# Windowed attention and a gated feed-forward in one kernel: half units, finer score bursts, and a planned choice of engines

## The chip, the cores and the metric

The kernel runs on one core of one Trainium2 chip. A core has five engines with a queue of instructions each, taken in order: PE (TensorE, matmuls), DVE (VectorE), ACT (ScalarE), POOL (GpSimd) and SP (SyncE, which here only starts DMA transfers). They meet through semaphores. PE and the vector engines exchange data through PSUM, eight banks of 128 x 512 fp32; everything else lies in SBUF, 128 partitions wide. The metric is the device time of one execution in microseconds (us), the median of several runs.

## The reference

Attention with a causal window of 64 positions, eight batches, eight heads, 576 positions, head size 64, all fp32; its output is the input of a feed-forward of width 1024 with a three-tap convolution along the sequence as a gate. The three weights arrive as 64-bit floats.

```python
def _attn_ref(q, k, v) -> np.ndarray:
    scores = scale * np.matmul(q, k.transpose(0, 1, 3, 2))
    mask = (rel >= 0) & (rel < window)
    scores = np.where(mask, scores, -1000000000.0)
    attn = np.exp(scores - np.max(scores, axis=-1, keepdims=True))
    attn = attn / (np.sum(attn, axis=-1, keepdims=True) + 1e-09)
    return np.matmul(attn, v).astype(np.float32)

def _moe_ref(x, w_in, conv_w, w_out) -> np.ndarray:
    h = np.maximum(x @ w_in, 0.0)
    ...
    for k in range(K):
        conv_out += conv_w[k][None, None, :] * hp[:, k:k + S, :]
    gate = 1.0 / (1.0 + np.exp(-conv_out))
    return (h * gate @ w_out).astype(np.float32)
```

## The kernel before

The 8 x 576 = 4608 positions are cut into twelve **units** of 384 (six blocks of 64, `NT`), u = 0 to 11. A unit passes through two parts.

**Attention.** `softmax` handles twelve pairs (head group g, block t) in three **bursts** of four (`NB`). `qk` (L347) multiplies queries and keys into PSUM on PE, `row_max` (L360, DVE) adds the mask and takes the row maximum, `exps` (L369, ACT) computes the exponentials, two instructions for each block, with the row sum beside, `guard` and `reciprocal` prepare the divisor, `normalise` (L382) multiplies, on DVE for units 0 to 2 and on POOL later. The probabilities are then turned. For units 0 and 1 ("wide", `BY_PE`) PE transposes them (`transpose_pe`, L389) and ACT copies them back (`untile`, L394). For the later units DVE transposes squares of 32 (`transpose`, L410) and small DMAs bring them to their place (`place`). `values` (L484) multiplies with v, one of four column groups c at a time; `split_hi` (ACT) and `split_lo` (DVE) write the result x as the sum of two reduced-precision numbers, xh and xl.

**Feed-forward** (`moe`, L573). The 1024 columns of DFF are eight steps f of 128. `mm1` (L505) computes one step as twelve matmuls of 128 x 128 by 384 columns (four c, three products: xh times the high weight, xh times the low one, xl times the high one) into one of two `acc` banks. `relu` (ACT) brings it to `hbuf`. For each pair i of steps `carry` (POOL) brings over the columns at the unit's edge, `conv_mid` (ACT) and `conv_side` (DVE, twice) form the convolution, `sig` (ACT), `gate` (DVE), `gate_hi` (ACT) and `gate_lo` (DVE) make the gated values gh and gl. `mm2` (L565) multiplies them with w_out into four banks `po`, summing over all eight steps; it runs about five steps (`LAG`) behind mm1. Then `po` is copied out (L607, L609) and stored.

**Weights.** Each of the sixteen chunks (eight of w_in, eight of w_out, 128 x 512) is loaded as 64-bit words of 0.5 MB into a staging tile, `bits`, of which there are two (each two chunks wide, and overlapping the tiles T of the transposes and of the output). `to_f32` (L248) turns them into fp32: ACT takes the absolute value of the high words (L252), POOL a maximum with a tiny number (L253), DVE shifts (L254) and puts in the sign (L256), ACT scales the low words (L259), DVE adds them (L260). `weights` then rounds to the high part (POOL for w_in, L277, ACT for w_out, L275) and DVE subtracts for the low part (L278). All eight steps of unit 0 come before unit 1, so all sixteen chunks are needed within unit 0.

**Order.** Every operation is a `Work` with a due time t (the tables START) and a cost. `queued` (L61) simulates the five engines with these costs and writes out the order in which each engine's instructions are issued; on the chip each queue then runs in that order and waits where data is late. Where the simulated PE would stand still in the first 110 us, `keep_busy` (L209) puts in matmuls on a tile of zeros (L216). ACT needs a table load when it changes between exponential and sigmoid (ACT_TABLE_LOAD in the profile).

Of the kernel before, what the change touches and what calls it, by code (L numbers as in the profile page):

```python
# [28 lines left out]
LAG = 5  # L29
BY_PE = 2  # L30
NB = 4
NBU = 2 * NT // NB
MASKED = -8.0e9
TINY = 2.0 ** -15

LAST = NU - 1
# [10 lines left out]

class Work:


    def __init__(self, t, eng, cost, do, r, w, kind, mb, port):
        self.t, self.eng, self.cost, self.do, self.r, self.w, self.kind, self.mb = t, eng, cost, do, r, w, kind, mb
        self.port = port
        self.needs, self.after, self.ready = 0, [], 0.0
        self.start = self.end_ = 0.0


def queued(works, fill=None):  # L61

    import heapq
    writer, readers = {}, {}
    for x in works:
        deps = set()
        for k in x.r:
            if k in writer:  # L70
                deps.add(writer[k])
        for k in x.w:
            deps.update(readers.get(k, ()))
            if k in writer:
                deps.add(writer[k])
        deps.discard(x)
        for d in deps:
            d.after.append(x)
        x.needs = len(deps)
# [4 lines left out]
    free = {"PE": 0.0, "DVE": 0.0, "ACT": 2.0, "POOL": 0.7, "SP": 1.3}  # L84
    state = dict.fromkeys(free)
    waiting = {e: [] for e in free}
    touched = {k: ("", 0.0) for k in [("sc", 0)] + [("acc", i) for i in range(2)] + [("po", i) for i in range(NC)]}
    for x in works:
        if x.needs == 0:
            waiting[x.eng].append(x)  # L90
    dma, port, order, left = 0.0, {"DVE": 0.0, "POOL": 0.0}, [], len(works)
    while left:
        best = None
        for e, ws in waiting.items():
            if not ws:
                continue
            start = max(free[e], min(x.ready for x in ws))
            if best is None or start < best[0]:
                best = (start, e)
        start, e = best  # L100
        x = min((x for x in waiting[e] if x.ready <= start),
                key=lambda x: x.t - (0.5 if x.kind and x.kind == state[e] else 0.0))
        if x.port:
            if e == "POOL" and start < port["DVE"]:
                free[e] = port["DVE"]
                continue
            start = max(start, port["POOL"])
            port[e] = start + x.port
        waiting[e].remove(x)
        if fill and e == "PE" and start < FILL_TO:  # L110
            t = max(free[e], FILL_FROM)
            n = int((start - t) * FILL)

            clean = [(end, k) for k, (by, end) in touched.items() if by != "PE" and end < t]
            if n > 0 and clean:
                order.append(Work(x.t, e, 0.0, fill(n, min(clean)[1]), [], [], None, 0, 0.0))
        turn = SWITCH[e] if e in SWITCH and (x.kind != state[e] if e == "PE" else x.kind and x.kind != state[e]) else 0.0
        if turn and e == "PE" and not x.kind:
            turn = LEAVE
        if e == "PE" or x.kind:  # L120
            state[e] = x.kind
        end = free[e] = start + turn + x.cost * (1.75 if e == "PE" and start < WARM else 1.0)
        if x.mb:
            dma = max(dma, start) + x.mb * 2.7
            end = dma + 1.9
        for k in x.r + x.w:
            if k in touched:
                touched[k] = e, end
        order.append(x)
        left -= 1  # L130
        for y in x.after:
            y.needs -= 1
            y.ready = max(y.ready, end + (0.0 if e == "PE" else 0.06) if y.eng == e else end + 0.2)
            if y.needs == 0:
                waiting[y.eng].append(y)
    return order

START = {  # L140
    "v0": -34.213,
    "pv0": -15.486,
    "conv": -34.622,
    "bits": ((-44.162, -48.108), (-49.962, -46.523)),
    "qk1": -44.058,
    "v1": -6.318,
    "qk2": 0.918,
    "qk0": (-88.698, -55.197, -55.435),
    "ex0": (-38.484, -35.539, -25.91),
    "sc1": (-35.664, -14.916, -14.661),  # L150
    "ex1": (-10.948, -3.722, -2.234),
    "mask": -13.894,
    "sig": ((5.143, 6.743, 8.637, 10.624), (2.954, 4.077, 7.59, 9.996), (4.046, 6.806, 8.285, 10.314)),
    "in": (-40.063, -38.679, -33.327, -12.569, -5.818),
    "out": (-5.241, -4.847, 7.996, 9.148),
# [13 lines left out]
def attention_moe(ctx: ExitStack, tc: tile.TileContext, q, k, v, w_in, conv_w, w_out, out):  # L169
# [56 lines left out]
    def two(t, eng, cost, do, **kw):  # L226
        at(t, eng, cost, do, port=cost, **kw)
# [74 lines left out]

    def wide(u):
# [429 lines left out]
```

## Time and profile before

| | |
|---|---|
| median of 3 runs | 529.05 us (527.6 to 529.41) |
| the profiled execution, its span | 528.6 us |
| busy: PE, DVE, ACT, POOL | 507.8, 377.7, 384.5, 105.5 us |
| matmuls (PE instructions) | 5646 |
| moved by DMA | 69.94 MB |

The span is that of one execution taken by the profiler. Busy time counts an engine's instructions only, not its waits; a busy PE may also be running at a lower clock, or on filler matmuls. A group's row reads: line, engine, operation, what is written and read, shapes, count, then total busy time, mean duration in ns, and the idle time just before these instructions with what ended it. In the chain of waits each piece of time belongs to what the end was waiting for. A row of the timeline begins with start and duration.

### The profile page before, as it was taken

To read this page: it belongs to the slowest core of one execution; us is meant where nothing else is said; L and a number is where in the kernel's file an instruction comes from. 1 tells how busy PE (TensorE), PEld (TensorE's weight loads), DVE (VectorE), ACT (ScalarE), POOL (GpSimd) and SP (SyncE) were. 2 spreads that over 40 slices of the span, in tenths; PEclk is the share of its full clock that TensorE was granted. 3 is DMA by queue.
4 is the path that set the end of the run, shared out by engine and by line. 5 is a ranking of instruction groups with operands and counts; after the bars stand their busy time and mean duration, and the time that the engine had idled before them with its cause. 6 is when DMAs were issued, how large, how long until landed. Compare 5 with 4: busy or idle time off the path is not lost.

```text
span 528.6 us, 14478 instructions
## 1 busy us (share of the span) xinstructions
PE 507.8 (96%) x5646; PEld 486.1 (92%) x5646; DVE 377.7 (71%) x1084; ACT 384.5 (73%) x1017; POOL 105.5 (20%) x192
## 2 busy tenths in 40 slices
PE   6867899999999999999999999999999999999996
PEld 4657799999899999999999999999999999999996
DVE  3998999998668676667767767767767767655552
ACT  1988999788795994696696697687687687544541
POOL 5663645112011120011021021021021021000000
PEclk9998999999999999999999999999999999999999
DMA  8982670265472264172173073083073053010011
GB/s 275 378 276 101 231 258 2 51 203 190 115 269 68 66 206 129 56 275 69 40 288 77 22 256 112 23 287 97 14 279 99 24 165 95 13 61 1 1 61 60
DMA packets 29459, 69.94 MB, mean 132 GB/s; under 512 B 5712, under 2 KB 17616, under 8 KB 29392
## 3 DMA queue, kind: packets, MB, share of 16 engines
q1 hardware_dynamic: 29392, 69.03, 39.6%
q8 instruction: 44, 0.72, 0.6%
q14 instruction: 23, 0.19, 0.1%
HBM read 47.73 MB, written 9.47 MB: 108 GB/s over the span
## 4 chain that ended last, share of the span: by engine, by line
PE 89%; DMA 4%; ACT 3%; DVE 2%; issue 1%; SPq 0%; ACTq 0%
PE po L571 39%; PE acc L508 38%; PE acc L488 6%; PE sc L357 5%; DMA q<-in_q_dram 2%; DMA T<-in_w_in_dram 1%; DVE s L364 1%; ACT ub L396 1%; ACT s L374 0%; ACT w L252 0%; DVE wil L278 0%; DVE w L260 0%; DVE xl L495 0%; DVE s L385 0%; ACT L374 0%
## 5 line engine op out<-in xcount | busy, mean ns | idle before, releaser
L508 PE MATMUL acc<-xh,wih 128*128 128x384 f32 x384 | 132.2, 344 | 1.8 <-ACT hbuf L529 0.9
L542 DVE SCALAR_TENSOR_TENSOR c<-hbuf,cw,c 128x386 f32<-128x386 f32 (+1 forms) x192 | 110.0, 624 | 32.8 <-ACT c L535 32.7
L571 PE MATMUL po<-gh,woh 128*128 128x386 f32 (+1 forms) x384 | 132.3, 345 | 0.0
L508 PE MATMUL acc<-xh,wil 128*128 128x384 f32 x384 | 130.9, 341 | 0.0
L508 PE MATMUL acc<-xl,wih 128*128 128x384 f32 x384 | 130.6, 340 | 0.0
L571 PE MATMUL po<-gh,wol 128*128 128x386 f32 (+1 forms) x384 | 129.8, 338 | 0.0
L571 PE MATMUL po<-gl,woh 128*128 128x386 f32 (+1 forms) x384 | 129.8, 338 | 0.0
L374 ACT ACTIVATE s<-s,nm 128x96 f32<-128x96 f32 (+2 forms) x288 | 105.4, 370 | 5.1 <-DVE nm L364 4.9
L508 PEld LDWEIGHTS acc<-xh,wih 128*128 128x128 f32 x384 | 72.9, 190 | 3.5 <-issue 2.1
L562 DVE TENSOR_TENSOR gl<-c,gh 128x772 fp32r<-128x772 f32 (+1 forms) x48 | 54.9, 1144 | 28.6 <-ACT gh L558 28.3
L571 PEld LDWEIGHTS po<-gh,woh 128*128 128x128 f32 x384 | 72.2, 188 | 2.9
L508 PEld LDWEIGHTS acc<-xl,wih 128*128 128x128 f32 x384 | 73.0, 190 | 0.0
L508 PEld LDWEIGHTS acc<-xh,wil 128*128 128x128 f32 x384 | 72.9, 190 | 0.0
L385 POOL TENSOR_TENSOR s<-s,r 128x768 f32<-128x768 f32 x27 | 39.7, 1471 | 165.4 <-DVE r L380 154.1
L554 DVE TENSOR_TENSOR c<-c,hbuf 128x772 f32<-128x772 f32 (+1 forms) x48 | 47.0, 980 | 36.0 <-ACT c L549 35.9
L571 PEld LDWEIGHTS po<-gl,woh 128*128 128x128 f32 x384 | 72.3, 188 | 0.0
L571 PEld LDWEIGHTS po<-gh,wol 128*128 128x128 f32 x384 | 72.3, 188 | 0.0
L529 ACT ACTIVATE hbuf<-acc 128x384 f32<-128x384 f32 x64 | 30.8, 484 | 46.2 <-PE acc L508 45.9
L549 ACT ACTIVATE c<-c 128x772 f32<-128x772 f32 (+1 forms) x48 | 40.7, 848 | 27.4 <-DVE c L542 27.2
L364 DVE CUSTOM_DVE_ANT_0 s<-sc,mask 128x96 f32<-128x96 f32 (+2 forms) x272 | 51.6, 254 | 9.0 <-POOL mask L328 5.3
L374 ACT ACTIVATION_READ_ACCUMULATOR s<-s,nm 128x1 f32 x288 | 55.2, 192 | 0.0
L535 ACT ACTIVATE c<-hbuf,cw 128x386 f32<-128x386 f32 (+1 forms) x96 | 53.6, 609 | 0.0
(64 smaller groups left out, 576.2 us busy)
## 6 DMA issues: line engine op xcount, KB each, us to landing
v<-in_v_dram SPq DMA_DIRECT2D x24, 768.0 KB, 7.1
ub<-T SPq DMA_DIRECT2D x240, 48.0 KB, 2.0
k<-in_k_dram SPq DMA_DIRECT2D x22, 448.0 KB, 5.6
q<-in_q_dram SPq DMA_DIRECT2D x22, 384.0 KB, 5.8
out_dram<-T SPq DMA_DIRECT2D x8, 772.0 KB, 4.4
T<-in_w_in_dram SPq DMA_DIRECT2D x8, 512.0 KB, 6.9
T<-in_w_out_dram SPq DMA_DIRECT2D x8, 512.0 KB, 5.1
out_dram<-T SPq DMA_DIRECT2D x3, 768.0 KB, 6.2
```

The source lines that it names most:

```text
L364: nc.vector.tensor_tensor_reduce(out=ss[b][:, i, h, o:n], in0=banks_of(u, b)[h][:, i * P + o:i * P + n], in1=mask[m][:, o:n], scale=-0.125 ...
L374: nc.scalar.activation(x, x, AF.Exp, bias=nms[b][:, e], scale=-1.0, accum_out=sms[b][:, e])
L385: on.tensor_tensor(sv, sv, rs[b].unsqueeze(2).broadcast_to([P, 2 * NB, n]), ALU.mult)
L488: nc.tensor.matmul(acc[bank(("v", u, c))][h * D:(h + 1) * D, t * W:(t + 1) * W], vs[:, c, t, h], ub[g][:, 2 * p:2 * p + 2, 2 * t + h], sta ...
L508: nc.tensor.matmul(acc[bank(("m", u, f))][:, :NX], w[:, f, c], x[u % 2][:, c], start=(c == 0 and j == 0), stop=(c == NC - 1 and j == 2))
L529: nc.scalar.activation(hbuf[:, f, o:o + NX], ps[:, :NX], AF.Relu)
L535: nc.scalar.activation(cs[i % 2][:, a, :n], hbuf[:, f, 1:1 + n], AF.Copy, scale=cw[:, 1, f:f + 1])
L542: nc.vector.scalar_tensor_tensor(c, hbuf[:, f, e:e + n], cw[:, e, f:f + 1], c, op0=ALU.mult, op1=ALU.add)
L549: nc.scalar.activation(c, c, AF.Sigmoid)
L554: nc.vector.tensor_tensor(c, c, hbuf[:, 2 * i:2 * i + 2, 1:1 + n], ALU.mult)
L562: nc.vector.tensor_tensor(gls[ring(u, i)][:, :, :n], cs[i % 2][:, :, :n], ghs[ring(u, i)][:, :, :n].bitcast(F32), ALU.subtract)
L571: nc.tensor.matmul(po[o][:, :n], w[:, f, es], x, start=(f == 0 and j == 0), stop=(f == NF - 1 and j == 2))
```

## The change

The whole body is rewritten around a plan; these are its parts.

- **Half units.** Units 0 and 1 run the feed-forward in two halves of DFF each, in turn: unit 0 steps 0 to 3, unit 1 steps 0 to 3, unit 0 steps 4 to 7, unit 1 steps 4 to 7 (`TASKS`). Each half sums its own `po` banks and copies them out. The first half is stored; the second is added to it in DRAM by an accumulating DMA that POOL issues (`store_more`). xh and xl of both units are held until then. Eight more copies out of PSUM result.
- **Bursts of two.** For units 0 and 1 a burst is two pairs instead of four (`FINE`, `bursts`), six bursts a unit. Their q and k come from one new input, `first`, laid out so that one DMA of 0.33 MB brings all that a burst needs.
- **Decoding.** Each chunk has a tile of its own (`raws`), loaded ahead and decoded through one of two work tiles `wx`; the high and low parts then take the place of the raw words (same tag). `to_magnitude` scales by 2^-112 within the absolute value, and the maximum on POOL goes away. Loads of the head keep one order on SP (`in_turn`).
- **Engines.** `CHOICE` names, per operation and unit (units 4 to 11 share one entry), the engine for `conv_mid`, `gate`, `gate_lo`, `relu`, `split_hi`, `normalise`, `guard`, `larger` (the rounding to the high part), `lo` and the copies out. In units 4 to 11 all four gates, one gate_lo, two conv_mid and one normalise go to POOL, two relus and all four split_hi to DVE.
- **Order.** `plan` lists the operations with an occupancy and a latency for each, `backward` finds a latest start for each from the end, `OFF` shifts some of these, and `schedule` writes out the queues, sticking to one kind of matmul or one ACT table (`STICK`). PSUM is one set of eight banks, given out by the plan (`Group`): scores, acc and po as before, with more of them for the first unit. mm1 is one piece of twelve matmuls instead of two of six.

```diff
+SPLIT = 2
+TASKS = [(0, 0, 4), (1, 0, 4), (0, 4, NF), (1, 4, NF)]
+LAG = 5
+TASKS += [(u, 0, NF) for u in range(SPLIT, NU)]
...
+def bursts(u):
+    k = NB // 2 if u < FINE else NB
+    return [tuple(range(n, n + k)) for n in range(0, 2 * NT, k)]
...
+    def decode(key, fs):
...
+        at("ACT", 0.03 + 0.5 * n, 0.14 + 0.5 * n, "magnitude", args, r=raw, w=[kx])
+        at("DVE", 0.07 + 0.267 * n, 0.15 + 0.267 * n, "shift", args, w=[kx], lock=0.07 + 0.267 * n)
+        at("DVE", 0.07 + 0.532 * n, 0.15 + 0.532 * n, "sign", args, r=raw, w=[kx], lock=0.07 + 0.532 * n)
+        at("ACT", 0.03 + 0.5 * n, 0.14 + 0.5 * n, "low", args, w=[k + ("lw",) for k in raw])
+        at("DVE", 0.07 + 0.532 * n, 0.15 + 0.532 * n, "add_low", args, r=raw + [k + ("lw",) for k in raw], w=[kx], lock=0.07 + 0.532 * n)
...
+        on({"ACT": (a, a + 0.11, 0.0), "DVE": (d, d + 0.08, d), "POOL": (p, p + 0.06, p)}, "larger", args, r=[kx], w=his + raw)
+        on(two(512, n), "lo", args, r=[kx] + his, w=[(key, f, "l") for f in fs])
...
+    for k, (u, f0, f1) in enumerate(TASKS):
+        if u not in done:
+            done.add(u)
+            attention(u)
...
+        for f in range(f0, f1):
+            need("in", f)
...
+        if part == "more":
+            at("POOL", 1.2, 1.2, "store_more", (u, k % 2), r=[("ot", k % 2, o) for o in range(NC)], w=[("out", u)], mb=1.8)
+        elif u != LAST:
+            load("store", (u, k % 2), 1.0, [("out", u)], r=[("ot", k % 2, o) for o in range(NC)])
...
+def in_turn(x):
+    return x.eng == "SP" and x.fn.startswith("load") and (x.fn == "load_w" or bool(x.args) and x.args[0] <= SPLIT)
...
+CHOICE = {
...
+    ('conv_mid', 1, 2): 'POOL', ('conv_mid', 1, 3): 'DVE', ('conv_mid', 2, 1): 'POOL',
+    ('conv_mid', 2, 2): 'POOL', ('conv_mid', 3, 2): 'POOL', ('conv_mid', 4, 0): 'POOL',
...
+    ('gate', 3, 0): 'POOL', ('gate', 3, 1): 'POOL', ('gate', 3, 3): 'POOL', ('gate', 4, 0): 'POOL',
+    ('gate', 4, 1): 'POOL', ('gate', 4, 2): 'POOL', ('gate', 4, 3): 'POOL', ('gate_lo', 0, 1): 'POOL',
...
+    @work
+    def load_first(u, b):
+        a, n, _ = first_at(b)
+        nc.sync.dma_start(qk[:, a:a + n], first[u, :, a:a + n])
...
-        at(t, "ACT", 0.0009 * n + 0.2, lambda: nc.scalar.activation(x, hw.bitcast(F32), AF.Abs), r=kb, w=kt)
-        at(t, "POOL", 0.0027 * n + 0.02, lambda: nc.gpsimd.tensor_scalar(x, x, TINY, None, op0=ALU.max), w=kt, port=PORT_CL)
+    def to_magnitude(x, hw):
+        nc.scalar.activation(x, hw.bitcast(F32), AF.Abs, scale=2.0 ** -112)
...
+    @work
+    def store_more(u, t):
+        nc.gpsimd.dma_start(out[u], ots[t], accum_op=ALU.add)
```

More of the change, by code (lines that the diff above doesn't have):

```diff
@@ L83, in queued @@
             readers.setdefault(k, []).append(x)
[L84 to L87, printed above, removed]
+        if x.grp:
+            x.grp.left += 1
+ENGINES = "PE", "DVE", "ACT", "POOL", "SP"
+HOP = 0.035
+ENTER, EXIT = 0.095, 0.14
+TABLE = 1.295
+LANES = 8
+def in_turn(x):
+    return x.eng == "SP" and x.fn.startswith("load") and (x.fn == "load_w" or bool(x.args) and x.args[0] <= SPLIT)
@@ L88, in queued, with schedule @@
+def schedule(works, prio, fill=False):
+    turns = sorted((x for x in works if in_turn(x)), key=lambda x: prio[x])
+    follows = dict(zip(turns[1:], turns))
+    issued = set()
+    n = {x: len(x.before) for x in works}
+    ready = dict.fromkeys(works, 0.0)
+    free = {"PE": 1.3, "DVE": 0.9, "ACT": 0.75, "POOL": 0.75, "SP": 0.75}
+    kind = {"PE": None, "ACT": None}
+    waiting = {e: [] for e in ENGINES}
+    bank = dict.fromkeys(range(8), 0.0)
+    left = {}
+    start = {}
     for x in works:
-        if x.needs == 0:
+        if x.grp:
+            left[x.grp] = left.get(x.grp, 0) + 1
+            x.grp.banks = None
+        if n[x] == 0:
@@ L118, in queued @@
[L118 to L122, printed above, removed]
-        if x.mb:
[L124 to L128, printed above, removed]
+            if any(bank[i] is None for i in t):
+                continue
+            at = max(bank[i] for i in t)
@@ L129, in queued @@
         order.append(x)
-        left -= 1
         for y in x.after:
-            y.needs -= 1
-            y.ready = max(y.ready, end + (0.0 if e == "PE" else 0.06) if y.eng == e else end + 0.2)
-            if y.needs == 0:
+            n[y] -= 1
+            same = y.eng == e and not x.mb
+            ready[y] = max(ready[y], s + occ if same else end + HOP)
+            if n[y] == 0:
                 waiting[y.eng].append(y)
[L136 to L155, printed above, removed]
[3 rows of a table removed]
-}
@@ new lines, in gate, with gate_hi, gate_lo, mm2 @@
+    @work
+    def gate(u, i, j, on):
+        engine[on].tensor_tensor(both(u, j), both(u, j), hbuf[:, 2 * i:2 * i + 2, 1:1 + width_of(u)], ALU.mult)
+    @work
+    def gate_hi(u, i, j):
+        nc.scalar.copy(ghs[j % 3][:, :, :width_of(u)], both(u, j))
+    @work
+    def gate_lo(u, i, j, on):
+        n = width_of(u)
+        engine[on].tensor_tensor(gls[j % 3][:, :, :n], both(u, j), ghs[j % 3][:, :, :n].bitcast(F32), ALU.subtract)
+    @work
+    def mm2(u, f, o, j, start, stop, bank):
+        n, a = width_of(u), f % 2
+        gh, gl = ghs[j % 3][:, a, :n], gls[j % 3][:, a, :n]
+        es = slice(o * P, (o + 1) * P)
+        for i, (w, x) in enumerate(((0, gh), (1, gh), (0, gl))):
+            nc.tensor.matmul(banks[bank[0]][:, :n], wts["out", f][:, w, es], x, start=(start and i == 0), stop=(stop and i == 2))
```

1093 lines of the change are left out of this document (714 added, 379 removed), and 3 rows, old and new, of the table START.

## The prediction

> **What bounds the kernel now.** I read the shares and the chain of waits of the page first, then the busy time of each engine by stage.
>
> ```profile
> PE 507.8 (96%) x5646; PEld 486.1 (92%) x5646; DVE 377.7 (71%) x1084; ACT 384.5 (73%) x1017; POOL 105.5 (20%) x192
> PE 89%; DMA 4%; ACT 3%; DVE 2%; issue 1%; SPq 0%; ACTq 0%
> ```
>
> PE is busy for 96% and carries 89% of the chain. So the end moves only by time in which PE does nothing useful, or by PE work itself. Where PE is idle, the stages show (length, busy time of each engine, clock, DMA):
>
> ```profile
> 0.00:4.71 4.71, 1.22 (x2) 0.53 (x3) 0.48 (x1) 1.28 (x1) 3.48 (x17) 1.00 0.61 172
> 4.71:37.44 32.73, 24.88 (x395) 19.79 (x396) 26.82 (x119) 25.16 (x99) 20.11 (x45) 1.00 0.90 329
> 37.44:70.00 32.56, 27.40 (x336) 25.05 (x337) 29.86 (x73) 27.64 (x67) 16.30 (x13) 0.90 0.58 197
> 70.00:131.60 61.60, 61.53 (x602) 60.14 (x601) 56.91 (x136) 54.84 (x142) 18.86 (x23) 1.00 0.39 129
> 131.60:453.00 321.40, 321.40 (x3835) 310.26 (x3834) 227.19 (x704) 243.79 (x657) 45.59 (x88) 1.00 0.41 129
> 453.00:524.40 71.40, 71.39 (x482) 70.37 (x480) 36.12 (x54) 31.48 (x54) 1.16 (x8) 1.00 0.06 24
> 524.40:528.60 4.20, 0.00 (x0) 0.00 (x0) 0.36 (x1) 0.32 (x1) 0.00 (x0) 1.00 0.50 171
> ```
>
> From 70 us on PE never pauses. All that can be won by better order lies before 70. "Busy" flatters that head: it counts filler matmuls (L216) and slow ones. I therefore price the useful PE work from the chain and the PE timeline (start, duration, what, count):
>
> ```profile
> 277.48 4.22 PE acc L508 x24
> 28.22 1.00 PE L357 MATMUL sc<-k,q 64*64 64x128 f32 x32
> 40.90 1.98 PE L391 MATMUL po<-ident,s 128*128 128x128 f32 x16
> 57.99 1.76 PE L488 MATMUL acc<-ub,v 128*64 128x64 f32 x48
> 256.21:296.46 40.25, 40.25 (x483) 38.92 (x484) 28.56 (x88) 30.41 (x82) 5.65 (x11) 1.00 0.41 132
> ```
>
> A big matmul takes 4.22/24 = 0.176 us; mm1 and mm2 have 2304 of them: 405. A settled unit takes 40.25, of which 192 x 0.176 = 33.8 are these, so 6.5 are attention; ten units have it: 65. The two wide units need six bursts of scores at 0.95 (one takes 1.00 and overlaps the next a little), twelve turns at 0.43 (sixteen transposes are four turns, 1.73 to the next start) and four pairs of values at 1.65: 17.5. Useful work is 487.5. So 528.6 = 4.7 until the first score + 487.5 + 4.2 after the last matmul + **32.2 lost**. Where:
>
> ```profile
> 37.44 0.41 PE L508 MATMUL acc<-xh,wih 128*128 128x384 f32 x1 [0.84 <-DVE xl L495]
> 45.87 1.16 PE L357 MATMUL sc<-k,q 64*32 64x96 f32 x64 [1.95 <-DVE nm L364]
> 47.95 0.66 PE L508 MATMUL acc<-xh,wih 128*128 128x384 f32 x1 [0.93 <-ACT hbuf L529]
> 48.41 0.52 PE L508 MATMUL acc<-xh,wil 128*128 128x384 f32 x1
> 62.94 0.92 PE L488 MATMUL acc<-ub,v 128*64 128x64 f32 x24 [2.29 <-DVE xl L495]
> L508 PE MATMUL acc<-xh,wih 128*128 128x384 f32 x28 | 11.0, 394 | 1.8 <-ACT hbuf L529 0.9 <-DVE xl L495 0.8
> ```
>
> The first mm1 starts at 37.44. Before it PE does six bursts of wide scores, six turns, four values and one burst of unit 2: 12.5 useful of 32.7, so 20.2 lost. After it, 12.0 remain lost. The last row groups L508 between 37.4 and 70.85: 3 x 28 matmuls, 14.8 us of work in 33 us. There PE waits for scores to be read, for relu, for unit 1's split, and runs matmuls of 0.52 instead of 0.34 after such gaps. Why the first mm1 is so late, the rows of ACT and POOL tell:
>
> ```profile
> 6.91 0.35 ACT L374 ACTIVATE s<-s,nm 128x64 f32<-128x64 f32 x1 [4.90 <-DVE nm L364]
> 13.05 0.68 ACT L252 ACTIVATE w<-T 128x512 f32<-128x512 f32 x1 [5.37 <-DMA T<-in_w_in_dram]
> 13.64 0.39 ACT L374 ACTIVATE s<-s,nm 128x128 f32<-128x128 f32 x1
> 14.03 0.39 ACT L374 ACTIVATE s<-s,nm 128x128 f32<-128x128 f32 x1
> L374 ACT ACTIVATE s<-s,nm 128x128 f32<-128x128 f32 (+1 forms) x41 | 15.8, 396 | 4.9 <-DVE nm L364 4.9
> 13.83 1.49 POOL L253 TENSOR_SCALAR w<-w 128x512 f32<-128x512 f32 x1 [3.74 <-ACT w L252]
> 26.50 1.06 ACT L396 COPY ub<-po 128x512 f32<-128x512 f32 x2
> ```
>
> After one block ACT stands 5.37 us behind a weight decode whose data has not come, and unit 0's exponentials queue behind it. Between 7 and 37.4 ACT does 41 exponentials; unit 0 has only 24. The rest are unit 1's, done ahead of unit 0's last splits.
>
> **The change, part by part.** *Order of the head (first loads, bursts of two blocks, half units).* Only what unit 0 needs has to precede its first mm1. On ACT that is 24 exponentials at 0.385 (14.03 - 13.64) = 9.2, six unturns at 0.47 (1.06 for two, overlapped) = 2.8, and two chunks decoded, four passes of 0.56 (13.64 - 13.05 less overlap) = 2.3, three splits 1.3: 15.6. Begun at 6.9 that ends at 22.5. Splitting the last values takes 2 to 3 more (row 62.94: PE waits 2.29 for one split). I take the **first mm1 at 25**, from 22 (ACT never idle) to 30 (the wait of 5.4 returns). By 25, at the 329 GB/s of the row 4.71:37.44, 6.7 MB can land; unit 0's q, k, v and four chunks are 5.7 MB by the shapes, so the loads fit narrowly. PE's useful work by then: unit 0's 8.7 (three pairs of bursts, six turns, two pairs of values) and some 1.9 of unit 1's scores. Lost before the first mm1: 25 - 4.7 - 10.6 = 9.7 in place of 20.2, **-10.5**.
>
> *Halves of DFF.* Unit 0 now runs four steps f, then unit 1 runs four, before any weight of the second half is needed. What that saves of decoding by then:
>
> ```profile
> L256 DVE SCALAR_TENSOR_TENSOR w<-T,w 128x1024 uint32<-128x1024 uint32 x7 | 8.5, 1216 | 0.0
> L254 DVE TENSOR_SCALAR w<-w 128x1024 uint32<-128x1024 uint32 x7 | 5.4, 766 | 0.0
> L278 DVE TENSOR_TENSOR wol<-w,woh 128x1024 fp32r<-128x1024 f32 x4 | 4.9, 1215 | 0.0
> L252 ACT ACTIVATE w<-T 128x1024 f32<-128x1024 f32 x7 | 8.0, 1150 | 2.7 <-DMA T<-in_w_in_dram 2.7
> L253 POOL TENSOR_SCALAR w<-w 128x1024 f32<-128x1024 f32 x7 | 24.8, 3540 | 12.3 <-ACT w L252 12.3
> L374 ACT ACT_TABLE_LOAD x20 | 25.7, 1283 | 1.1 <-PEq L727 0.7
> L529 ACT ACTIVATE hbuf<-acc 128x384 f32<-128x384 f32 x64 | 30.8, 484 | 46.2 <-PE acc L508 45.9
> ```
>
> A pair of chunks costs DVE about 1.2 + 0.8 + 1.2 + 1.2 = 4.4 (L260 adds a pass like L256) and ACT 2.3. Eight chunks, 17.6 of DVE and 9.2 of ACT, move behind unit 1's first half. But unit 1's attention is now due after four steps, not eight. Its ACT work is 9.2 + 2.8 + 1.7 for splits = 13.7, with two more decodes (2.3) and four relus (1.9) before it ends: 22.5 + 17.9 = 40.4, some 43 with the last splits. PE has from 25 on 8.4 of unit 0's mm1 and about 6.8 of unit 1's attention: until 40. So a gap of 3 stands there, and I take as much again for the first conv chains, whose sigmoid costs ACT two table loads of 1.28 among the exponentials. **6 lost in place of 12.0: -6.** Ends: 0 (all of it covered) and 12 (the same waits under other names). From some 52 us on unit 0's second mm1 steps are ready as filler, and PE is the bound as it is now from 70.
>
> *Decoding in place, without the maximum.* The maximum leaves POOL: 24.8 us for seven pairs, each step between two of DVE. Its own share of the gain is in the terms above; nothing is added. The weights no longer wait for two staging tiles (bits), so their loads can run ahead; the price is that they queue before q, k, v. That is the 30 above.
>
> *Adding in DRAM.* Units 0 and 1 write their sums twice: eight more copies from PSUM and two accumulating DMAs issued by POOL. The trace has none, so: below, nothing, as no later step reads out; above, one plain store of the same size each, 4.4 us from issue to landing, if POOL stands for all of it and a gate behind it is late. I take 0: the nearest row, the store on SP, has nothing behind it that PE needs, and POOL is 20% busy.
>
> ```profile
> out_dram<-T SPq DMA_DIRECT2D x8, 772.0 KB, 4.4
> L562 DVE TENSOR_TENSOR gl<-c,gh 128x772 fp32r<-128x772 f32 (+1 forms) x20 | 25.0, 1248 | 14.8 <-ACT gh L558 14.8
> L562 DVE TENSOR_TENSOR gl<-c,gh 128x772 fp32r<-128x772 f32 x5 | 4.8, 963 | 3.8 <-ACT gh L558 3.8
> L385 POOL TENSOR_TENSOR s<-s,r 128x768 f32<-128x768 f32 x15 | 22.1, 1471 | 99.4 <-DVE r L380 99.4
> L554 DVE TENSOR_TENSOR c<-c,hbuf 128x772 f32<-128x772 f32 x36 | 35.3, 982 | 26.4 <-ACT c L549 26.4
> L277 POOL CAST wih<-w 128x1024 fp32r<-128x1024 f32 x3 | 3.4, 1144 | 5.6 <-DVE w L260 5.6
> ```
>
> *Engines from the plan, units 2 to 11.* PE's instructions per unit stay; I take their time as unchanged, within 0.25 a unit for one change of tile shape more or less (2.5 in ten units). ACT loses two conv_mid, two relus, four splits: from 30.4 it only falls. DVE loses four gates and one gate_lo (4 x 0.98 + 1.2 = 5.1) and gets six PSUM reads and two normalisations, about as much: 28.6 stays. POOL gets five operations of 1.47 for two of them, and two conv_mid whose scaling the trace does not show on POOL (for 772 elements from 0.9 each, by the copy of L277, to 2.7, by L253; I take the copy's, as it is one pass too): 5.65 + 5 x 1.47 - 2 x 1.47 + 1.7 to 5.4 = 11.8 to 15.5 of 40.25. All fit under PE, so 0.
>
> **Sum**: 4.7 + 487.5 + 9.7 + 6 + 4.2 = **512.1** against the profiled 528.6. The runs' median, 529.05, lies 0.4 above that execution: **512.5**.
>
> The Trainium skill, "TensorE: Matmul & The Clock Gate", part on the clock gate, says that the array falls to half clock only after an idle window of about 3.4 us. By that rule short gaps would cost only themselves. This trace differs: after gaps of 1.95 and 0.93 the matmuls at 48.41 last 0.52, so gaps in the new head can cost again what they last.
>
> **Rivals.** *A: unit 1 too late.* If ACT again stands behind a decode for its data, some 8 us come back and the halves buy little: 520, up to 526. For it: ACT's queue is in order, and 5.37 + 2.7 of such waits are there now. Against: the weights come into tiles of their own. *B: nothing gained*, half the head merely renamed, 527.5 to 530.6: would need both terms to fail. *C: slower, DVE bound by POOL in the settled units.* Where POOL holds DVE off for its whole time, DVE needs 28.6 - 1.1 + 11.8 to 15.5 = 39 to 43 of 40.25; at 43 PE waits 2.7 in each of ten units: 512.5 + 27 = 539. It decides from 40.25 of DVE per unit. Against it: beside 3 x 1.47 = 4.4 of POOL per unit gate_lo takes 1248 instead of 963, 1.1 a unit, a quarter of POOL's time; scaled to 13 it is 3.3, DVE 31. The Trainium skill, "SBUF — State Buffer", section "Who interferes with whom", has it as an exclusive lock: a DVE operation with two SBUF inputs and one of GpSimd that reads SBUF block each other fully. By that rule C's condition is nearly met; the rows here show a quarter. *D: PE work itself shrinks* by one change of shape per unit and the head packs fully: 503.
>
> **How the numbers follow.** Chances: forecast (506 to 520) 0.62, A 0.19, D (below 506) 0.06, B 0.04, C 0.09. The range 504 to 525 holds the forecast, most of A and half of D. A measurement of this kernel tells about 0.3% (1.6 us) from no change: faster is forecast, A and D, 0.87; same 0.04; slower 0.09.
>
> **What would show it.** Right: the first mm1 near 25; ACT without a wait of 5 us on DMA in the first 15; PE without pause from about 55 instead of 70; a settled unit at 40.2. Wrong: settled units longer than 40.5 with PE waiting for gl or gh (C); a wait of over 5 us on unit 1's split before its mm1 (A); matmuls of 0.5 after 45 us.

## The result, and the profile after

The changed kernel takes 547.48 us (median of four runs, 546.71 to 549.71), the kernel before beside it 528.75: a ratio of 1.0375, interval 1.0344 to 1.0406. The forecast was 512.5; the change is **slower**. The profiled execution spans 545.7 us, 33.6 more than the sum of the prediction.

The shares and the chain of waits of the changed kernel, from its page:

```profile
PE 510.7 (94%) x5631; PEld 479.5 (88%) x5631; DVE 405.9 (74%) x1148; ACT 335.4 (61%) x914; POOL 236.8 (43%) x295
PE 48%; DVE 24%; SPq 9%; ACT 7%; DMA 5%; POOL 4%; issue 3%; DVEq 0%; POOLq 0%; ACTq 0%
```

PE carried 89% of the chain before; now it carries 48% and DVE 24%. POOL works 131 us more, ACT 49 less. By stage (stretch, its length, busy time of PE, weight loads, DVE, ACT, POOL, clock, DMA share, GB/s):

```profile
0.00:14.00 14.00, 10.63 (x103) 6.95 (x107) 8.52 (x52) 8.06 (x34) 9.92 (x50) 1.00 0.77 260
14.00:25.00 11.00, 6.74 (x129) 5.26 (x122) 8.07 (x47) 8.59 (x37) 3.85 (x7) 1.00 0.99 380
25.00:34.20 9.20, 5.28 (x116) 3.95 (x113) 9.13 (x23) 9.20 (x31) 1.44 (x3) 0.97 1.03 409
34.20:70.00 35.80, 33.23 (x426) 30.23 (x424) 34.85 (x96) 31.17 (x89) 16.92 (x19) 0.91 0.56 209
70.00:135.40 65.40, 57.57 (x625) 54.75 (x624) 64.52 (x161) 41.45 (x111) 33.92 (x32) 0.97 0.38 123
135.40:508.60 373.20, 365.19 (x4075) 347.14 (x4074) 262.34 (x750) 224.23 (x598) 157.63 (x178) 1.00 0.37 116
```

Two things are to be seen. From 25 to 135.4 us **DVE** is busy 108.5 of 110.4 us and looks like the new bound (experiment 6 tests that). And from 135.4 to 508.6, where the kernel before had PE busy to the last hundredth, PE now stands still for 8.0 us.

To split the loss I use a mark that both kernels pass: the moment at which PE has done 384 of the 2304 large matmuls (two units' worth), and the moment of 2112 (eleven), counted over PE's records (all 2304 are in both traces). The stages above were cut at 135.4 and 508.6, within 2 us of the marks.

```
                                   before   forecast   after
first mm1                            37.4       25.0    34.2
two units' worth done               130.6      114.1   135.1
a unit, mean of the next nine        40.0       40.0    41.3
from eleven units to the end         38.0       38.0    39.0
span                                528.6      512.1   545.7
```

So 21.0 of the missing 33.6 us lie ahead of the first mark, 11.6 (nine units by 1.29) in the settled part and 1.0 behind it. Of the 11.6, 8.0 are pauses of PE; the other 3.6 lie within its busy time and were not taken apart. The first mm1, which the prediction put at 25, starts at 34.20. First PE's timeline (start, duration, what, count, and in brackets the wait before it), then two rows of DVE's:

```profile
21.30 0.67 PE L881 MATMUL bank<-qk 64*64 64x128 f32 x16 [2.96 <-DMA qk<-in_first_dram]
28.59 0.56 PE L881 MATMUL bank<-qk 64*64 64x128 f32 x16 [1.44 <-DMA qk<-in_first_dram]
33.32 0.95 PE L881 MATMUL bank<-qk 64*64 64x128 f32 x16 [1.85 <-DVE xl L977]
34.20 1.01 PE L984 MATMUL bank<-xh,w_in 128*128 128x384 f32 x2
35.01 0.52 PE L984 MATMUL bank<-xl,w_in 128*128 128x384 f32 x1
```

```profile
30.46 2.30 DVE L790 CUSTOM_DVE_ANT_0 wx<-raw_in,wx 128x1024 uint16<-128x1024 uint16 x3
32.69 1.01 DVE L977 TENSOR_TENSOR xl<-bank,xh 128x384 fp32r<-128x384 f32 x2
```

All three bursts are unit 1's. The first two wait for their own load and stand in PE's queue ahead of unit 0's last turns and its last values: there late data of unit 1 holds up unit 0. The third ends its wait with DVE's split of unit 0's values (L977), which the first mm1 needs as well; that split came behind 2.30 us of decoding (L790) in DVE's queue. What changed on DVE and POOL, by groups (line, engine, operation, shapes, count, busy time, mean ns, idle time before), here of the changed kernel, with the same convolution step of the kernel before in the second fence:

```profile
L1034 DVE SCALAR_TENSOR_TENSOR c<-hbuf,cw,c 128x386 f32<-128x386 f32 (+1 forms) x192 | 137.7, 762 | 37.1 <-POOL c L1026 26.4
L1042 POOL TENSOR_TENSOR c<-c,hbuf 128x772 f32<-128x772 f32 (+1 forms) x42 | 74.3, 1769 | 113.2 <-ACT c L1038 113.2
L1026 POOL TENSOR_SCALAR c<-hbuf,cw 128x386 f32<-128x386 f32 (+1 forms) x44 | 61.2, 1395 | 84.2 <-ACT hbuf L1010 47.2
```

```profile
L542 DVE SCALAR_TENSOR_TENSOR c<-hbuf,cw,c 128x386 f32<-128x386 f32 (+1 forms) x192 | 110.0, 624 | 32.8 <-ACT c L535 32.7
```

The same 192 instructions of `conv_side` take 27.7 us more, beside a POOL that is busy more than twice as long. And `conv_mid` takes POOL 2 x 1.395 = 2.79 us for two segments; the kernel's plan has 0.82 for it. That made the plan itself a suspect: `schedule` gives a start to every instruction, and the trace has the real one. The plan ends at 511.6 us (its last matmul and 4 us for what follows it), close to my own sum, though it has the first mm1 at 30.25 and two units' worth at 116.0; the chip falls behind it like this (median over the instructions of DVE and ACT planned within 4 us of that time):

```
planned time       20    40    60    90   120   200   280   480
chip later by     3.4   5.5  12.9  15.7  20.9  25.8  27.2  32.5

us per operation                 plan    chip
conv_mid, POOL (two segments)    0.82    2.79
gate, POOL                       1.50    1.77
conv_side, DVE (two segments)    1.06    1.52
first loads, us per MB           2.45    3.8 (260 GB/s until 14 us)
```

Three theories came from this. **P**: the queues were written for prices that the chip doesn't have; in a fixed order every late instruction holds up those behind it. **Q**: POOL slows DVE directly, as rival C had it. **R**: the new structure (halves, sums in DRAM, finer bursts) itself costs time.

### The profile page after: what moved, and what is told of

It reads as the page before. It is cut to its first block, busy times and chain, and to the rows that moved or that the text cites. A ratio compares the mean times of both kernels' runs of the same rounds, so it can differ in the third digit from the quotient of the medians.

```text
span 545.7 us, 14378 instructions
## 1 busy us (share of the span) xinstructions
PE 510.7 (94%) x5631; PEld 479.5 (88%) x5631; DVE 405.9 (74%) x1148; ACT 335.4 (61%) x914; POOL 236.8 (43%) x295
## 4 chain that ended last, share of the span: by engine, by line
PE 48%; DVE 24%; SPq 9%; ACT 7%; DMA 5%; POOL 4%; issue 3%; DVEq 0%; POOLq 0%; ACTq 0%
PE bank L1059 22%; PE bank L984 19%; SPq L960 8%; DVE c L1034 7%; PE bank L967 4%; PE bank L881 3%; ACT s L912 3%; DMA qk<-in_first_dram 3%; POOL c L1026 2%; DVE gl L1051 2%; DVE T L947 2%; DVE s L928 2%; DVE s L902 2%; DVE wx L790 2%; DVE xl L977 2%
## 5 line engine op out<-in xcount | busy, mean ns | idle before, releaser
L984 PE MATMUL bank<-xh,w_in 128*128 128x384 f32 x768 | 200.9, 342 | 8.5 <-DVE hbuf L1012 5.6
L1059 PE MATMUL bank<-gh,w_out 128*128 128x386 f32 (+1 forms) x768 | 201.0, 343 | 3.2 <-ACT ot L1064 1.6
L1034 DVE SCALAR_TENSOR_TENSOR c<-hbuf,cw,c 128x386 f32<-128x386 f32 (+1 forms) x192 | 137.7, 762 | 37.1 <-POOL c L1026 26.4
L984 PEld LDWEIGHTS bank<-xh,w_in 128*128 128x128 f32 x768 | 139.9, 191 | 12.9 <-DVE hbuf L1012 7.1
L1059 PEld LDWEIGHTS bank<-gh,w_out 128*128 128x128 f32 x768 | 137.7, 188 | 7.4 <-ACT ot L1064 2.3
L1059 PE MATMUL bank<-gl,w_out 128*128 128x386 f32 (+1 forms) x384 | 130.4, 340 | 1.5 <-DVE gl L1051 1.5
L984 PE MATMUL bank<-xl,w_in 128*128 128x384 f32 x384 | 130.6, 340 | 0.0
L1042 POOL TENSOR_TENSOR c<-c,hbuf 128x772 f32<-128x772 f32 (+1 forms) x42 | 74.3, 1769 | 113.2 <-ACT c L1038 113.2
L1026 POOL TENSOR_SCALAR c<-hbuf,cw 128x386 f32<-128x386 f32 (+1 forms) x44 | 61.2, 1395 | 84.2 <-ACT hbuf L1010 47.2
L1059 PEld LDWEIGHTS bank<-gl,w_out 128*128 128x128 f32 x384 | 72.4, 188 | 2.5 <-DVE gl L1051 2.4
L984 PEld LDWEIGHTS bank<-xl,w_in 128*128 128x128 f32 x384 | 73.5, 191 | 0.7 <-DVE xl L977 0.6
```

What stands on the lines that cost most here:

```text
L984: nc.tensor.matmul(banks[bank[0]][:, :NX], w[:, a, c], y[x][:, c], start=(c == 0 and j == 0), stop=(c == NC - 1 and j == 2))
L1026: engine[on].tensor_scalar_mul(c, h, w)
L1034: nc.vector.scalar_tensor_tensor(c, hbuf[:, f, e:e + n], cw[:, e, f:f + 1], c, op0=ALU.mult, op1=ALU.add)
L1042: engine[on].tensor_tensor(both(u, j), both(u, j), hbuf[:, 2 * i:2 * i + 2, 1:1 + width_of(u)], ALU.mult)
L1059: nc.tensor.matmul(banks[bank[0]][:, :n], wts["out", f][:, w, es], x, start=(start and i == 0), stop=(stop and i == 2))
```

## The experiments

**1. Other engines, the same queues: Q alone.** The plan stays; only at emission an operation goes to another engine at its old place in the program (e1: `conv_mid` from POOL to ACT; e2: `gate` and `gate_lo` from POOL to DVE; e3: both).

```diff
+            args = x.args
+            if x.fn == "conv_mid" and args[-1] == "POOL":
+                args = args[:-1] + ({"conv_mid": "ACT"}.get(x.fn, "DVE"),)
```

> Every conv_mid that the plan gave to POOL runs on ACT instead, at the same place of the same written order; nothing else moves. Port theory (POOL's conv_mid takes 1.4 us an instruction where the plan has 0.4, holds conv_side back from 0.62 to 0.76 us and delays the chain to the gate): about half of the 18.7 us lost comes back, 536 to 541, conv_side near 0.68, settled units 40.8 instead of 41.5. Order theory (the written order of the head and of PE's pieces costs the time): 546 to 549, since ACT only gets fuller by 2.2 a unit.

> Every gate and gate_lo of POOL runs on DVE instead, same written order. Port theory (POOL's 1.77 us gates also hold the port): conv_side falls to 0.69, but DVE gets about 4.5 us a unit more of its own, so 538 to 545. Order theory: DVE, which is full from 60 to 140 us, becomes later still: 548 to 556.

> conv_mid to ACT and gates to DVE together, same written order. Port theory: conv_side back at 0.62, settled units at 40.3 to 40.5, the time 530 to 535, what is left above before being the head. Order theory: 545 or more.

Measured: 548.44, 547.89 and 550.34 us, ratios 1.0385, 1.0383 and 1.0423 (1.0401 to 1.0444). The group of `conv_side` in e3:

```profile
L1034 DVE SCALAR_TENSOR_TENSOR c<-hbuf,cw,c 128x386 f32<-128x386 f32 (+1 forms) x192 | 114.3, 648 | 26.5 <-ACT c L1024 26.4
```

With 163 us of POOL's work gone (236.8 to 74.2), `conv_side` is nearly as short as before (648 against 624 ns), and the kernel is not faster: DVE got the gates in exchange, and nothing in the queues knew of it. e1 and e3 lie where the rival theory, the order, had them, and e2 just under its range. Contention is real, but alone it doesn't explain the time.

**2. Without halves: R.** Units 0 and 1 run all eight steps at a time.

```diff
-TASKS = [(0, 0, 4), (1, 0, 4), (0, 4, NF), (1, 4, NF)]
+TASKS = [(0, 0, NF), (1, 0, NF)]
```

> Units 0 and 1 run all eight steps each, no halves, no sums added in DRAM; engines and all the rest as planned, and the plan writes its order anew. If the halves themselves cost time (second copies, unit 1's attention due after four steps): faster than after by 3 or more, 540 to 544. If they bring something in the head that is lost elsewhere: slower, 550 to 556. If neither: 546 to 549.

Measured: 556.8 us, ratio 1.0542 (1.0519 to 1.0565); two units' worth done at 144.6 instead of 135.1. The halves **save** 9 us. R is wrong for them. The 9 may flatter them, as engines and shifts had been searched with the halves in place; the plan itself has 16.

**3. The plan's prices, one at a time: P.** e5 puts POOL's prices right (the two-operand work 18% higher, besides the line below) and leaves all engines as chosen; e8 keeps `conv_mid` off POOL; e6 gives the settled units their engines of before and no shifts (OFF); e7 charges 3.7 us per MB for loads in the first 15 us.

```diff
-                on({"ACT": (1.02, 1.12, 0.0), "DVE": (0.55, 0.63, 0.55), "POOL": (0.82, 0.88, 0.82)}, "conv_mid", (u, i, j),
+                on({"ACT": (1.02, 1.12, 0.0), "DVE": (0.55, 0.63, 0.55), "POOL": (2.6, 2.7, 2.6)}, "conv_mid", (u, i, j),
...
-            dma = max(dma, s + 0.3) + x.mb * 2.45
+            dma = max(dma, s + 0.3) + x.mb * (3.7 if s < 15 else 2.45)
```

> Engines as in after; only the prices from which the plan writes its order are set to what the trace shows for POOL: a conv_mid 2.6 instead of 0.82, gate, gate_lo and lo 18% more. Theory of wrong prices (queues written for times that POOL doesn't keep, so instructions stand behind late ones): 538 to 543, and the lag behind the plan's own times shrinks. Theory that POOL's share itself is the cost, or that the head is: 545 to 550, as the chip does the same work on the same engines.

> No conv_mid on POOL anywhere; the plan writes its order anew with them on ACT. Exchanging the engine alone (first run of this study) gave nothing. Theory of wrong prices: the order now fits, 535 to 541. Theory that the head and the settled units lose for other reasons: 545 to 550.

> Units 4 to 11 get back the engines of before (conv_mid, relu, split_hi on ACT, gates on DVE, normalise on POOL) and no shifted starts; the head is that of after. If the settled units' choice of engines costs their 1.4 us a unit: 41.7 goes to 40.3 to 40.6, the time to 534 to 538. If it is the way in which this plan orders a settled unit: 41.5 or more stays, 545 to 552.

> In the plan a megabyte loaded before 15 us is priced at 3.7 us instead of 2.45 (the trace moved some 260 GB/s there, not 408); nothing else. If the head's loss begins with loads that land later than planned (PE and ACT wait 6.1 and 4.2 us for them): first mm1 at 31 to 32 instead of 34.2, and 3 to 6 us of the time, 541 to 544. If not: 546 to 549; a new order of the rest may move it by a few us either way.

Measured: e5 552.27 (ratio 1.0467), slower still, though its plan now knows the price: the engines and shifts were chosen for the old one, and its own plan ends at 529. That lies above both of its ranges, and against P in its plain form: true prices alone, with the old choices, don't help. e8 539.5 (1.0223, 1.0199 to 1.0247), **8 us better**. e6 543.6 (1.0298), 4 better, between its two ranges, and from 120 us on it falls only 2 us further behind its plan, where the changed kernel falls 12. e7 545.31 (1.0344, 1.0311 to 1.0378), 2 better at most (the intervals overlap), but the chip keeps to that plan within 1.4 us until 60 us, and the first mm1 comes at 31.3 instead of 34.2.

**4. Together, and two parts alone.** e9 is e6, e7 and e8 in one; e10 also takes the gates and the decoding off POOL in the head; e11 goes back to bursts of four (FINE = 0); e12 drops all the shifts (OFF = {}).

> The three edits that helped, at once: no conv_mid on POOL, loads before 15 us priced at 3.7 us a megabyte, units 4 to 11 with the engines of before. Alone they gave 8.0, 2.2 and 3.9 us; the second half of the last is in the first. Theory that the loss is the plan's wrong prices at these places: 533 to 537, running less than 12 us behind its own plan (which promises 527 now, 511 for after). Theory that what is left is POOL holding DVE in the head: 537 or more, units 0 to 3 as late as now.

> As the run before, and gate, gate_lo, lo and the rounding leave POOL in units 0 to 3 as well; only normalise and guard stay there. Contention theory: conv_side falls to 0.62 us from the start and the kernel runs within 8 us of its plan (532): 535 to 540. Theory that the head is bound by DVE's own work: the work that comes back makes it later, 540 to 546.

> Units 0 and 1 in bursts of four pairs, three a unit, instead of two; the rest as in after. The plan itself expects the first mm1 9 us later and the end 8 later. If the finer bursts bring the head forward on the chip too: first mm1 at 38 to 43, 551 to 557. If the loads set the head in any case: first mm1 at 35 to 37, 545 to 550.

> Control for how far a new order alone moves the time: all shifted starts (OFF) dropped, engines and prices as in after. The plan expects 9 us more. If the plan's small gains are real on the chip: 555 to 560. If they drown in what the plan prices wrongly: 545 to 552.

Measured: e9 540.05 (1.0221), e10 542.16 (1.0274): the gains don't add up, and both came out as the rivals had it (what is left is DVE in the head). The chip now keeps within 12 and 7.5 us of the plans (at 480 us), and the plans themselves end at 527 and 533. e11 550.09 (1.0427): with coarse bursts the first mm1 comes at 44.7, 10 us later and later than either theory had it, and the end only 2.6. e12 541.06 (1.0255, 1.0236 to 1.0275), below both of its ranges: without the shifts the plan ends 13 us **later** (524 against 511; the expectation had said 9, and for e11 8 where the plan has 11), and the chip is 6 us **faster**, though its first mm1 comes at 41.1. The shifts bring 13 us by the plan's count and cost 6 on the chip, as P would have it; a plan tuned too tightly at any prices could do the same. e10 shows what is left in the head without POOL, in stretches of 20 us (columns as above):

```profile
40.00:60.00 20.00, 16.87 (x229) 14.10 (x226) 19.80 (x43) 18.27 (x39) 4.01 (x8) 1.00 0.78 286
60.00:80.00 20.00, 19.06 (x166) 18.25 (x165) 19.93 (x62) 17.66 (x50) 2.00 (x3) 1.00 0.01 2
80.00:100.00 20.00, 20.00 (x227) 18.54 (x226) 19.79 (x56) 16.64 (x39) 4.48 (x8) 1.00 0.35 127
100.00:120.00 20.00, 16.69 (x276) 14.63 (x274) 18.78 (x69) 18.72 (x63) 0.23 (x2) 0.91 0.35 83
```

DVE is full even so: 78.3 of 80 us. Taking work off POOL unblocks DVE and gives it the same work back.

**5. Choices made anew for corrected prices.** START, CHOICE, OFF and STICK were searched again at random on the plan's own count, with the structure as it is. e13: POOL's prices and the early loads corrected. e15: `conv_side` too. e14: as e15, with 0.25 us instead of 0.035 from one engine's end to the start of what waits for it (HOP), so that the plan keeps a margin. e17 and e18: that margin only after 125 us (0.08 before), and 0.6 us more for PE's first work behind a pause, from two starts of the search. (The expectations give a plan's end without the 4 us. Worked out from the kernels, the plans' last matmuls end at 514.6 in e13, 517.2 in e14, 511.3 in e15, 514.9 in e17 and 515.5 in e18.)

```diff
-HOP = 0.035
+HOP = 0.25
...
-                    at("DVE", 1.064, 1.15, "conv_side", (u, i, j, e), r=hs + ["cw"], w=[c], lock=1.064)
+                    at("DVE", 1.2, 1.29, "conv_side", (u, i, j, e), r=hs + ["cw"], w=[c], lock=1.2)
...
+            if s > WARM and s - free["PE"] > 0.8:
+                extra += 0.6
```

> The changed kernel with three of its plan's prices put to what the chip showed (conv_mid of two segments on GpSimd 2.6 us instead of 0.82, the other arithmetic on GpSimd 15% more, a load before 15 us at 3.7 us per MB instead of 2.45), and START, CHOICE, OFF and STICK chosen anew for those prices by a random search on the plan's own count of time; the halves, the sum in DRAM, the scores of two blocks and the decoding in place stay. By the corrected plan it ends at 515 us (the old START, CHOICE and OFF end at 537 by it). Theory (the change loses since its queues and engines were chosen for prices that the chip does not have): the chip keeps within 5 to 13 us of this plan, 520 to 528, ratio 0.985 to 1.00, first mm1 at 31 to 35, units 2 to 11 at 40.5 to 41 a unit. Rival (the structure itself loses, halves and the two extra sums with everything on VectorE earlier): VectorE runs behind again from 40 us and the chip falls back 20 to 30 us, 535 to 545, as in the runs with corrected prices and old shifts.

> As the run with corrected prices and choices made anew, with two more corrections before the search: conv_side of two segments 1.2 us instead of 1.06, and 0.25 us instead of 0.035 from the end of one engine's work to the start of what waits for it on another, so that the plan keeps a margin. Its own plan ends at 519. Theory (what was left over was thin margins: PE paused 3.2 us between 75 and 255 and 3.1 between 255 and 455 because each step was due exactly when it was wanted): PE pauses under 3 us from 75 on, units 5 to 11 at 40.3 to 40.8, end 522 to 529. Rival (the structure: VectorE is the bound of the first 135 us and can't be relieved without GpSimd in its way): two units of large matmuls done at 130 to 132 as in the run before, settled units as there, 534 to 538.

> The same with conv_side at 1.2 us but without the margin (0.035 us from engine to engine). Its own plan ends at 513. By the theory of margins it falls behind its plan by 15 to 20 us, 528 to 533, and comes out behind the run with the margin; by the rival the two come out alike.

> The two last corrected runs put together and searched again: corrected prices, conv_side at 1.2 us, from engine to engine 0.08 us before 125 us and 0.25 after it, and 0.6 us more for PE's first work behind a pause of over 0.8 us (matmuls run at half speed there). The search began from the head of the run without margin and the settled units of the run with margin. Its plan's last matmul ends at 515. Theory (what the choices can win back is the margin in the settled units and a head as early as the run without margin): two units' worth done at 129 to 133, a unit at 40.3 to 40.6, the chip 10 to 15 us behind the plan, 528 to 533, level with the kernel before at best. Rival (head and settled units trade with each other): 534 to 537 as the two runs apart.

> The same from another start of the search (the whole run without margin), its plan's last matmul at 515.5, first mm1 planned at 30.5. It tells how far two plans that are alike by the count differ on the chip: by the theory both lie within 3 us of each other, 528 to 533.

```
                     us    ratio (interval)          behind its plan   two units'   a unit,
                                                     at 90, at 480     worth done   next nine
changed kernel     547.48  1.0375 (1.0344, 1.0406)     15.7   32.5       135.1        41.3
e13                536.96  1.0158 (1.0120, 1.0196)      6.4   16.8       131.2        40.7
e15                533.85  1.0115 (1.0082, 1.0149)      7.3   18.8       129.4        40.8
e14, margin        536.63  1.0162 (1.0111, 1.0214)     10.5   13.8       135.9        40.2
e17, margin late   536.08  1.0132 (1.0067, 1.0197)      8.4   13.6       137.7        39.7
e18, margin late   533.08  1.0085 (1.0059, 1.0112)      3.9   11.5       132.6        40.1
before                                                                   130.6        40.0
```

New choices, with the structure as it is, win back 14 of the 19 us (547.48 to 533.08): most of the loss lies in engines and order. That they were bad because the prices were wrong, as P says, fits the lag behind the plan but isn't shown apart, since no run searched anew with the old prices. None beats the kernel before. The expectations were missed in part: e13 and e14 ended where the rival had them (e14 though its settled units are as short as the theory asked), and e15, without the margin, came out level with e14 or ahead of it (the intervals overlap) and not behind. PE's busy time from 130 to 250 and from 255 to 455 us, in the changed kernel, in e15 and in e14:

```profile
130.00:250.00 120.00, 113.75 (x1222) 107.74 (x1230) 88.91 (x236) 71.87 (x182) 50.71 (x61) 1.00 0.39 112
255.00:455.00 200.00, 197.62 (x2288) 187.74 (x2288) 140.11 (x420) 128.83 (x359) 89.98 (x100) 1.00 0.39 126
```

```profile
130.00:250.00 120.00, 115.00 (x1399) 108.70 (x1398) 91.56 (x269) 78.02 (x216) 56.21 (x60) 1.00 0.46 132
255.00:455.00 200.00, 198.42 (x2324) 190.66 (x2323) 156.30 (x459) 134.98 (x348) 62.52 (x83) 1.00 0.38 124
```

```profile
130.00:250.00 120.00, 120.00 (x1492) 114.56 (x1491) 93.88 (x294) 73.89 (x212) 40.43 (x49) 1.00 0.46 134
255.00:455.00 200.00, 198.90 (x2327) 191.23 (x2326) 159.12 (x458) 129.30 (x338) 29.10 (x57) 1.00 0.39 126
```

With the margin PE stands still 1.1 us in these 320, without it 6.6, in the changed kernel 8.6; DVE is fullest where PE waits least (253 us against 229). It isn't POOL's share either: e9, with less POOL than e14 (57 us against 70 in the two stretches) and no margin, takes 41.0 a unit, and e17, with 68.91 us of POOL from 255 to 455, 39.7. So in the settled units the loss is probably work that is due exactly when PE wants it and comes a little late. Two things hold this back from proof: the plans were searched apart, so they differ in more than the margin; and a kernel that is late at the first mark has more work ready behind it. At eleven units e14 and e15 are level (497.3 and 496.6): what the margin saved later it had cost before.

The last two don't decide it. e17 came out as the rival had it (536, two units' worth at 137.7), e18 where the theory's range ends (533.08, at 132.6 within 129 to 133). None has a head well ahead of the kernel before together with short units: two units' worth are done between 129.4 and 137.7 in all five, against 130.6 before, though one plan promised 120 (e15). The halves' 9 us are in these heads, and as much is lost in them again.

**6. Less work for DVE in the head.** The changed kernel, but in units 0 and 1 one of the two outer taps of the convolution is left out.

```diff
     def conv_side(u, i, j, e):
+        if u < 2 and e:
+            return
```

> The changed kernel as it is, but in units 0 and 1 one of the two outer taps of the convolution is left out: 16 instructions of VectorE of some 0.92 us, 14.7 us of its work before 135 us. Theory (VectorE is what the first 135 us wait for): two units of large matmuls are done 7 to 13 us earlier, at 122 to 128 instead of 135.4, and the end is 535 to 541. Rival (loads, ScalarE and the order bound the head, VectorE only looks full): 132 to 136, end 543 to 548.

Measured, a single run: 539.44 us, two units' worth done at 131.2. The end is where the theory has it, 8 us earlier; the mark moves by only 3.9 for 14.7 us of work, close to the rival's 132 to 136 and far from the theory's 122 to 128. The stretches of 20 us show why:

```profile
60.00:80.00 20.00, 16.23 (x140) 15.00 (x139) 19.93 (x57) 15.66 (x53) 7.95 (x9) 0.91 0.26 90
80.00:100.00 20.00, 20.00 (x174) 19.61 (x172) 16.49 (x39) 15.80 (x35) 11.71 (x12) 1.00 0.29 90
100.00:120.00 20.00, 18.80 (x301) 17.70 (x301) 18.74 (x59) 15.42 (x47) 11.05 (x12) 1.00 0.68 232
```

DVE is full until 80 us and has room from there (16.49, 18.74), while PE still pauses in two of the three stretches. So DVE is one bound of the head and not the only one. e18 says the same: DVE is busy 98.1 of the 107.6 us from 25 to 132.6 there, and PE still stands still for 13.3. What the other bounds are was not taken apart.

## Why the prediction was wrong

- **"First mm1 at 25 (22 to 30)", -10.5.** Measured 34.2, so 9.2 of the term is missing. The step counted ACT's work alone. The kernel's own plan, which counts every engine, has 30.25 here, so 5 of the 9 were lost on paper. ACT did lose its wait of 5 us (two waits for the weights, 4.2 together, are left, and one of 2.0 for the convolution's); but from 25 to 34.2 DVE is busy 9.13 of 9.20 us and PE waits for its split. My check of the loads, 6.7 MB at 329 GB/s, was sound in bytes (14 us at 260 and 11 at 380 are 7.8 MB) and blind to their order: PE waits 2.96 and 1.44 for scores of unit 1, queued ahead of unit 0's rest because the plan held them for landed. With the early loads at their true price (e7) the first mm1 comes at 31.3. That is above the 30 that I kept for a late load, so the early loads, with the order that follows from their price, are 3 of the 9 us, and DVE's queue most of the rest (argued from its rows; no run isolates it). The step also took for granted that the end follows the first mm1. It doesn't: in e11 the first mm1 comes 10.5 later and the end 2.6 later, in e12 it comes 6.9 later and the end 6.4 earlier.
- **"Halves: 6 lost instead of 12.0", -6.** Halves are worth 9 (e4), so mechanism and sign were right. The sentence behind it failed, that from 52 us PE is the bound as it was from 70. The rows that I had quoted say why: DVE had 0.48 + 26.82 + 29.86 + 56.91 = 114.1 us of work in the first 131.6, and the forecast has the same work done 16.5 earlier, by 115.1, with DVE never idle from the first microsecond. By the groups of both traces until the mark, the new engines take some 18 us from DVE there (gates, low parts, normalisation) and give it about as much (rounding, relu, splits, `conv_mid`). `conv_side` at 0.917 instead of 0.668 us and slower decoding made it 125.1 by 135.4. **This is the step that failed most**: I read the engine with long visible waits (ACT) as the limit, and never added up the other one. With 125.1 us of work the mark at 114.1 was out of reach; that it came at 135.1 and not at some 125 is not explained by DVE alone (experiment 6).
- **"All fit under PE, so 0".** PE's time per unit is 41.3, not 40.0: 11.6 in nine units. `conv_mid` on POOL was priced by a copy (0.9) and measures 2.79, just past my upper bound of 2.7, so POOL is busy 18.0 of each 40 us (89.98 in 200), above the 11.8 to 15.5 that I gave. DVE is at 28.0 of 40, as forecast. So the engines do fit, and yet PE waits: fitting by share doesn't mean being on time. With the margin a unit is back at 40.2, 39.7 and 40.1 (e14, e17, e18).
- **Rival C**, DVE full by POOL's blocking in the settled units, has the right sign and the wrong place: settled DVE is 70% busy, and the full DVE is in the head. Its size, "a quarter of POOL's time", was a mean over unlike cases. The tile's statistics (count, min/median/max in ns) show that most `conv_side` are as fast as ever and a few three times as long:

```profile
L1034 DVE SCALAR_TENSOR_TENSOR c<-hbuf,cw,c x192: 571/614/2075, 45.5 to 532.4; 128x386 f32<-128x386 f32 x144, 128x384 f32<-128x384 f32 x48
L1042 POOL TENSOR_TENSOR c<-c,hbuf x42: 1686/1702/2212, 59.9 to 534.0; 128x772 f32<-128x772 f32 x32, 128x768 f32<-128x768 f32 x10
L1026 POOL TENSOR_SCALAR c<-hbuf,cw x44: 1234/1262/2012, 49.8 to 521.1; 128x386 f32<-128x386 f32 x32, 128x384 f32<-128x384 f32 x12
```

  Set against POOL's records one by one, a `conv_side` lasts 0.61 us with no POOL beside it (102 of them). Beside POOL's two-operand gate alone (three) it lasts 1.92, 0.87 us more for each us of overlap; beside the one-operand `conv_mid` alone (25) only 0.18 more; and DVE's steps that read PSUM (relu beside a gate, ten) none. The Trainium skill, "SBUF — State Buffer", section "Who interferes with whom", says that a DVE instruction with two SBUF inputs and a GpSimd instruction that reads SBUF shut each other out. The trace agrees for the gate and is far milder for the scaling, where POOL is delayed too (below). I had weighed that rule as one factor for all of POOL; it holds pair by pair.
- **Decoding in place and adding in DRAM at 0**: PE waits for no accumulating store, whose landing takes 6.8 us. Decoding was not free: DVE's two passes over the raw words take 24.2 us for the sixteen chunks (L783, L790), 19.8 before (L256, L260), all of it in the head where DVE is full. No run tried either alone.
- **Clock.** I gave matmuls of 0.5 after 45 us as a sign of failure; the granted clock is 0.91 in the stretch from 34.2 to 70, where it was 0.90 before from 37.4 to 70, and 0.97 from there to 135.4, where it was 1.00. The traces, which have the clock from 23.6 us before and from 13.1 after, show it at half in stretches of 3.41 us, two before (from 47.5 and 64.5) and three after (from 33.6, 50.6 and 74.5). One more of them is 1.7 us of PE's full speed at most. What goes with it is not the single gap, as I had read the row at 48.41, but how busy PE was over a whole stretch: each of the five stands behind one of the same length in which PE was busy for less than half, 1.16 and 1.56 us before, 1.57, 1.17 and 0.44 after. Here the first, from the kernel before:

```profile
44.08:47.50 3.42, 1.16 (x64) 0.90 (x64) 3.42 (x20) 3.42 (x14) 2.42 (x3) 0.99 0.56 171
47.50:50.91 3.41, 2.96 (x9) 2.99 (x10) 3.41 (x6) 3.41 (x6) 0.00 (x0) 0.50 0.35 141
```

What stays open: whether a queue exists that brings two units' worth under 129 with this structure. The search says only that it found none that the chip kept to; its count still misses 4 to 10 us of the first 90.

## What to carry to other kernels

When a head is to be shortened, add up the work of every engine until the mark and set it against the new time; one that has no room is a new bound, whatever the present waits show. An order written from a plan is worth no more than the plan's prices: compare each operation's price with the trace, and how far the chip lags behind the plan over time, before tuning on it, since a search finds the errors of the prices first. Plans that end as early by the count differ on the chip by how much lateness they bear: a margin at each hand-over went with settled units at 40 here, but no run with it was clearly faster than the best without it (533.1 against 533.9).

## What the runs showed of the hardware that was not expected

- A scaling by a per-partition factor on POOL (L1026, 386 columns fp32) takes 1.26 us in the median, 3.3 ns a column, where no `conv_side` runs beside it (25 of 44), and 1.54 where one does (19). The two-operand gate takes 1.70 for 772 columns, 2.2 ns, with or without one, and the copy of 1024 columns in the kernel before 1.1 ns. One operand less is not faster there.
- POOL delays `conv_side` by 0.87 of the overlap in its gate and by 0.18 in its scaling (counts above), and DVE's relu, which reads PSUM, not at all.
- The granted clock falls to half for 3.41 us (at times for twice that) behind a stretch of 3.41 us in which PE was busy for less than about half. Counted in all twenty traces in stretches of that length at full clock, it fell behind 53, the busiest of which had PE busy for 0.55 of it; every stretch below 0.45 is among them.
- DMA moves 260 GB/s in the first 14 us and 380 to 409 from there to 34 us, with the DMA engines already at 0.77 in the first stretch.
